# First clusters assigned by two pairs of heads, eight more tiles turned by DMA, g(h) and a*b kept in SBUF, and a new order of work

## The chip, the cores and the metric

The kernel runs on one core of a Trainium2 chip. The metric is the device time of one execution in microseconds (us): the median of the runs. Instructions run on TensorE (PE), VectorE (DVE), ScalarE (ACT) and GpSimd (POOL), each with a list of its own that it works through in order; transfers are issued from the queues of SyncE (SP), ACT and POOL.

## The reference

Everything is float32. There are 2 batches of 8 heads, 768 tokens, 64 columns per head, and 16 clusters per head; the two mixtures that follow work on all 1536 tokens of 512 columns.

```python
# attention: a token looks only at tokens of its own cluster
q_assign = argmax(einsum('bhsd,hcd->bhsc', q/|q|, c/|c|), -1)    # k_assign likewise
scores = where(q_assign == k_assign, (q @ k.T) / 8, -1e9)
x = softmax(scores) @ v                 # heads side by side: 1536 x 512
# first part: w_in 512 x 2048, w_out 2048 x 512
h = x @ w_in
g = where(h >= 1, h, where(h <= -1, 0, (h + 1)**2 / 4))
x = g @ w_out
# second part: w1, w2 512 x 1024, w3 1024 x 1024, w_out 1024 x 512
h = ((x @ w1) * (x @ w2)) @ w3
out = h @ w_out
```

## The kernel before, in words

**The pieces.** Two heads make a pair, 2 x 64 = 128 rows of SBUF. A unit u (0 to 7) is a batch and a pair: 0 to 3 are batch 0, 4 to 7 batch 1. A unit has two groups of 384 query rows, and a group has six tiles (two heads, three times 128 query rows), so there are 96 tiles s of 128 query rows x 768 keys; 0 to 47 are batch 0.

**Precision.** A float32 operand is split into a high part (rounded) and a low part (what is left); a product is three passes, high x high, high x low, low x high (`PASSES`). The copies at L347 (ACT) and L349 (DVE) make high parts, the subtractions at L352 (POOL or DVE) low parts. The names `X`, `G`, `whl`, `k`, `q`, `phl` and `pt` are such pairs.

**The start.** The centroids are loaded, normed (L419 to L432) and turned (`cT`). All four pairs of k and of q of batch 0 are loaded into `kq0` on SP's queue. `a_mm` (L511) writes the cluster logits of all pairs into one PSUM tile `sc` of 768 columns, first for k and then for q, and `a_hot` makes one-hot rows in steps over 768 columns: turn in 32 x 32 blocks (L525), maximum over 16 clusters (L531), comparison with it (L538), turn back (L543), a product with the triangle `tri` on PE (L547), and the mask (L551). The mask goes to `mask0`, and `kq_fill` copies 16 rows of it per head by DMA into rows 64 to 80 of `kq2`. There a score of two different clusters gets a term so large that its exponential is zero. While PE has nothing else, `idle_mm` (L459) multiplies the identity with itself, 80 times.

**One tile.** `s_mm` (L798) makes scores in PSUM, first from `k` and `q`, then from `kq2` with the mask rows; `s_max` (L806) takes the row maximum on DVE, `s_bias` (L811) scales it on POOL, `s_exp` (L819) is the exponential P on ACT. P is then turned so that the keys lie on the partitions. Either on PE (`s_pT`, L836, six products with the identity into the tile's own PSUM), and then a copy out (L347 or L349, and L352 for a low part); or P stays in PSUM, is split into `phl` (two buffers in batch 1), and a DMA transpose (L866, on SP's queue) turns it into `pt`. `PE_EVERY = (1, 3)` says which: every tile of batch 0 and every third of batch 1 by PE. `pv` (L907 and L915) multiplies P with V for a group into `av`; there x is multiplied by 1/r and split into `X0`.

**The mixtures.** The tokens of batch 0 are block 0, those of batch 1 block 1. A product of block 0 is 12 matmuls of 384 columns (`mm4`, L1198) into one of the PSUM tiles `mo`: three of them in batch 1's attention, one before. Three steps follow for h: Relu into `tmp` (L1206), square (L1214, L1216), and `h_max` (L1222), which writes g(h) back into `mo`; then `add_split` makes the two parts of `G` from `mo` and frees it. `ab_mul` does the same with a*b. Block 1 uses sums of matrix quarters and seven half-size products instead of eight (L1450). The weights arrive as words of twice the size, and DVE and POOL make floats of them (L1051 to L1084); w3 and w_out of the second part are multiplied beforehand into `wp` (L1142).

**What sets the order.** The `add` calls list every piece of work with the engines it may run on. `ORDER` is a string in which two letters name one piece and which of its engines does it. `plan.order()` reads it, and the pieces are issued in that order, each engine's list in the same order. No scheduler runs when the kernel is built; the string is the whole order.

Of the kernel before, what the change touches and what calls it, by code (L numbers as in the profile page):

```python
# [38 lines left out]
    "##%%%(%*%:#*#,#%#8#(#4%#%@%>%<#<#@#B&*#.#0#2&8&-#L%,&(&>&;&F&7&D#c#P;@&0#R#6#a;N;Z;i%.#:#k%B&N&P&@#Z$(;J%0%2"  # L39
    "%4%6$2#J#y#_#e&4;B&T#u#|%D%8$6#F$B&<;u%i&L#D$0&H&X$P&.$:$@$%#i;P;]%F%H%J%L%N$Z$V$>;D&2;e;R;k#o$c$F;_&J;T$T$."  # L40
    "#X#s;F#q#H$J&B;V$4$D$y;m$|;X$L&V;w;H;L;o*H*J*L*a*T*V$H*X*m$<$u$_$m*c*e<,<:*o*q*Z#g#>$X$g$w;y;a*N$]#w$i;q*s*]"
    "$8#N;c*g$e;s*P;g<%<.$#*S*i#]$N$k$a#m*u*`<<<><@<H*k<D<B&R<F*y*|<T+,$,$R$q+.*w$*$o$s#T#V+H+#+%+(+T<0<2;|<J+0+2"
    "+4<4<L<N+*+6<6<8+8<#+a&k+J<(+@&Z<V+c+L+N+m+P+V+:+e<c<_<P<R<X<o+g+X&^&`<Z&f+Z+]+<+R+_+y&g<]<a+|+o+q+><e,,+i<q"
    "<*=%&s,#,%+s+u,(+l,.+B,0,2&v<g<i<k+D=8,4,H+F<s<u<w+w,*,6,a,T<y<|,J,L&a&c,@,V,c,X=(,N,P=:=H,Z=*&j,m=,=.=0,e,g"
    ",i,]<m=<,8,:=>=2,R=B,_,k=V=J,y,|-#,o,q=g=L=@=D=N-%,s=y=#=4=6-H-,,<,>=P-.-J-(,u%R=R=T=F,w>0=X-L-0-+-2&|=Z=]&z"
    "-N=a-a-T(6=i-8=_=c,B-V>>((>*-P-4-c=e-:,D,F=|-X-Z>2-e-S-7&q-g>4&m>#-m=k(-=m=o=q(*(2-]-i&o-@(.-_>H=u-o-q>%>6=s"
    "($-k&w>N>(>8-s>,(%.,-y(>(4-<->-|..-u.H(<>..J>@>B>a.#.0.%>q.2.4.(>D>:>F%P><=w-w-B>J>L>P?%.8.:(B.+-E.L.N.P(8>R"
    ">T>V>k?6.6(A>^>_%T-F>c>e>X>Z(0%k%m.T>s.@>g.V.X.Z>u>w>y.R>|?#(:?(?H>i>m.<.].a.>.c.e._.g(H.y.m>o?*.o.|/#.q?0?8"
# [24 lines left out]
    "OZO#O/P6P(9X9ZO%O(9R9T9]9_PsPX*@*BO0P8P:P<P+8y8|9a9cOHP>PuQ<P@PZP]*D*F9#PaPw9(9*9eOJOa9g9iOL9kOcP_PcPBQ>9mOf"
    "OgPDOiOkQXPg9s9u9w9y9oQFOn9qP,P0P2Oo:6PePyQ@QBPiPkQZP|Q#P.9|Q]Q%Q(:8PN:#:%:::<Q|:(QDQHQJ:DPPPmQ_Po:>:@:F:HR>"
    ":JQaPFPSQ*:B:RQMQN:0R#PH:LR,PJPT:T:NQcPr:P:*R@RBRa:V:XR%QhQi:aPL:,:.:2:c:Z:]:_:e:g:4QeQ,Q.QPQRR(RDR*R.Q0Q2Q4"
    "Q6RFR0R2R4:i:k:m;#QT:oQ8Q:RHRJ;%QkRLRk:qS#;(;*QV:s:uR6RNQmQsQo;2:x:y:|QqRc;,QuR9;.QwR:R<S.QyRPRmReRXS&RpS)Rg"
    "RRRZR^RUS@SJS];0;:SyT#TPTaT%RVRqRiR_;4;6;8RtT5TNS|T=TLTTS0S3RuRwSBRzT^T)T9;<T;T+S*S,S4S6S:SMSNTfSESFSH;>TRS="
    "S>TWT7T,T_R|SgTyT@S_SbSPSeT|U(U*TYT[V2TuTCSjU-SlThT/SVSsTdTqV4TDT1TGU0U4U9U;T3SSSXU=U.U@V;STS8SZTmU#TIV=U&VB"
    "T?VFU?V?V@VKScV6WDSvTKVIV9TpWFXVUDSmSoSqU3VMTiSwUFWHU7UHVVTlTtULWLUSUTUCVDXZUVTwUcUeUJUgUXWJUNUZUiVOVRVPU]Um"
    "U_UkWNWPUoUPUaUwUyX]UqXXVfU|V$UtWTWXW]WRV_V%VZViWZWiX|YiV(V*W_UuVTV,VXVgV.V]Y0WwX`VkXaV0XcWqVmVuVwVoVaWaWdW%"  # L80
    "WfXhXjXkYkWmVcVqVyW(W*XmY%XoV|WVW0XqXeW|VsW,W#WsX#W.YwZ,W2W4YmWoX*W:W<W>WkY#W6W8YoXtXuW@XBXEWBYsYyWyX%Y4X.X0"
    "Z:XwXyWgY~Z(Y2X(X8X:Z/X2X4Y@XFXHX<Z1XJZHZJYBX>X@WuX,YDZ*Z<Z?Z6YGXLYHX6Z#Z%ZQZXYqZMZRZNZTZV[Z[]Z^ZaYvY(Y*Y6Y8"
    "Y,Y<Y:YJXNXPZfYLXRZZZ_YNXTYPYTZ8Z@Z2Z4]m[`YRZjZk[bYVYXYZZD[d[e[gZgZCZdY.]%ZF[kZmZ|[mY>Y]]p]r[p[t[q[iY_]|YaZu"
    "ZqYcYeYg]5Zo^#^%^0[%[(](Zw[.]wZs]6[#[2[4^3^5[w[y[F]D[6[*[,[<[H]F]H[8^>[J[v^(]s^,[|[:^L]K]L[?^N__[L[N^A[@]y^*"
    "[B[D^U^C^P^]_a^.]*].Zy]8^S]$^V]u^X^[[0`q^a_h[P[R^f^g_i^:^6]:],^i]2^q^k]<[T]>a%[V_l^<_c^m]N[X]B]c^c]Q^8^D]0^H"
# [55 lines left out]
def cluster_attention_moe_kernel(  # L141
# [223 lines left out]


    LATE = 8.0
    W_AFTER = [("al",0,"q",3)]
    V_AHEAD = 4
    AHEAD = 16  # L370
    U_DVE = 4
# [1344 lines left out]
```

## Time and profile before

| | |
|---|---|
| median of the runs | 736.93 us (736.58 to 737.46, 3 runs) |
| the profiled execution | 738.52 us, its span 736.80 us |
| PE busy | 721.2 us, 98% of the span |
| DVE busy | 629.2 us, 85% |
| ACT busy | 445.2 us, 60% |
| POOL busy | 284.0 us, 39% |

The span is the stretch from the first to the last recorded instruction; 1.7 us of the execution lie around it. A view by stretches shows for each engine how long it was busy, and the clock granted to TensorE as a part of its full speed. The view of one engine in order of time shows each group of like instructions with its start, the time it took, and in brackets how long the engine stood before it and what ended that wait. The chain of waits follows the work that ended last back from step to step.

### The profile page before, as it was taken

The page shows a single profiled execution, that of the slowest core. Times are in us where ns is not written, and L with a number is a line of the kernel's source. Part 1 is how long each engine was busy: PE and PEld are TensorE (multiplying, and loading weights), DVE is VectorE, ACT ScalarE, POOL GpSimd, SP SyncE. Part 2 cuts the span into 40 slices and gives each one's busy share as a digit, 9 for nine tenths or more (in the row PEclk, how much of TensorE's full clock was granted, in tenths as well). Part 3 has the DMA queues.
Part 4 walks back from the last instruction along what each step waited for, and adds up shares of the span by engine and source line. Part 5 has one row for each costly group of instructions (what it writes and reads, how often), then busy time and mean ns, then how long its engine had stood idle before and what let it go on. Part 6 is the DMA issues. An engine that isn't in the chain of part 4 may idle for free.

```text
span 736.8 us, 12150 instructions
## 1 busy us (share of the span) xinstructions
PE 721.2 (98%) x4273; PEld 638.4 (87%) x4273; DVE 629.2 (85%) x1153; ACT 445.2 (60%) x836; POOL 284.0 (39%) x358
## 2 busy tenths in 40 slices
PE   6999999999989999999999999999999999999997
PEld 3976666566589999999999999999999999999997
DVE  6999988998878889999999998659988878999950
ACT  6589887767666678785886675323665435444311
POOL 4332235122433523463354424222744343178601
PEclk9999999999999999999999999999999999999999
DMA  8354777575486697888869796544131312221212
GB/s 330 102 185 137 204 239 236 187 221 205 135 157 179 131 177 205 181 213 215 223 178 249 205 206 181 130 151 147 47 94 50 101 44 73 67 62 58 87 49 81
DMA packets 100973, 112.76 MB, mean 153 GB/s; under 512 B 61488, under 2 KB 69680, under 8 KB 100912
## 3 DMA queue, kind: packets, MB, share of 16 engines
q1 hardware_dynamic: 78768, 52.48, 28.6%
q10 hardware_dynamic: 22144, 59.52, 26.9%
q8 instruction: 33, 0.54, 0.3%
q14 instruction: 28, 0.23, 0.1%
HBM read 73.70 MB, written 20.19 MB: 127 GB/s over the span
## 4 chain that ended last, share of the span: by engine, by line
PE 76%; DVE 2%; DMA 2%; ACT 2%; issue 0%; POOL 0%; ACTq 0%; DVEq 0%
PE mo L1198 35%; PE sc L1450 7%; PE sc L1198 7%; PE sc L798 6%; PE mo L1450 6%; PE av L915 3%; PE mo L1142 3%; PE sc L836 3%; PE av L1450 2%; PE av L1198 1%; DMA pt<-phl 1%; PE av L907 1%; PE mo L893 1%; ACT P L819 0%; DMA wd<-wf 0%; DMA wf<-wd 0%
## 5 line engine op out<-in xcount | busy, mean ns | idle before, releaser
L1198 PE MATMUL mo<-X,whl 128*128 128x384 f32 x900 | 165.8, 339 | 0.0
L1198 PEld LDWEIGHTS mo<-X,whl 128*128 128x128 f32 x900 | 157.2, 189 | 1.9 <-issue 0.9
L1198 PE MATMUL mo<-G,whl 128*128 128x384 f32 x660 | 121.6, 337 | 0.0
L1198 PEld LDWEIGHTS mo<-G,whl 128*128 128x128 f32 x660 | 114.9, 188 | 1.1 <-DVE wf L1061 0.3
L806 DVE TENSOR_REDUCE nm<-sc 128x1 f32<-128x768 f32 x96 | 89.7, 952 | 15.4 <-PE sc L798 14.0
L352 POOL TENSOR_TENSOR whl<-wf,whl 128x512 fp32r<-128x512 f32 x54 | 70.7, 1312 | 74.2 <-DVE whl L349 38.0
L1084 POOL TENSOR_TENSOR wf<-wf,w 128x512 int32<-128x512 int32 x32 | 42.6, 1332 | 84.3 <-DVE wf L1067 21.8
L819 ACT ACTIVATE P<-sc,nm 128x768 f32<-128x768 f32 x64 | 57.1, 897 | 18.6 <-POOL nm L811 11.4
L811 POOL TENSOR_SCALAR nm<-nm 128x1 f32<-128x1 f32 x96 | 24.0, 250 | 99.0 <-DVE nm L806 93.2
L1142 PE MATMUL mo<-wo,wf 128*128 128x512 f32 x128 | 57.8, 594 | 0.3 <-POOL wf L1084 0.3
L347 ACT ACTIVATE whl<-wf 128x512 fp32r<-128x512 f32 x68 | 42.5, 628 | 24.5 <-PE mo L1198 17.6
L798 PE MATMUL sc<-k,q 128*128 128x512 f32 (+1 forms) x192 | 55.1, 368 | 2.1 <-ACT pt L347 2.1
L347 ACT ACTIVATE pt<-sc 128x768 f32<-128x768 f32 (+1 forms) x53 | 41.8, 808 | 20.4 <-PE sc L836 16.7
L836 PEld LDWEIGHTS sc<-ident,P 128*128 128x128 f32 x384 | 43.7, 141 | 11.9 <-issue 4.6
L836 PE MATMUL sc<-ident,P 128*128 128x128 f32 x384 | 50.2, 274 | 2.2 <-ACT P L819 2.2
L798 PE MATMUL sc<-kq 80*128 80x512 f32 (+1 forms) x192 | 49.8, 341 | 0.1
L1051 ACT ACTIVATE wf<-w 128x512 f32<-128x512 f32 x64 | 42.5, 672 | 6.3 <-DMA w<-in_w_in_dram 4.2
L1198 PE MATMUL sc<-G,whl 128*128 128x384 f32 x252 | 46.0, 337 | 0.0
L1067 DVE SCALAR_TENSOR_TENSOR wf<-w,wf 128x512 uint32<-128x512 uint32 x64 | 44.6, 701 | 1.0
L1142 PEld LDWEIGHTS mo<-wo,wf 128*128 128x128 f32 x128 | 23.5, 190 | 24.2 <-issue 22.8
L1198 PEld LDWEIGHTS sc<-G,whl 128*128 128x128 f32 x252 | 44.2, 188 | 0.0
L352 POOL TENSOR_TENSOR wh<-ws,wh 128x256 fp32r<-128x256 f32 x44 | 33.5, 775 | 18.0 <-DVE wh L349 7.6
(222 smaller groups left out, 1496.6 us busy)
## 6 DMA issues: line engine op xcount, KB each, us to landing
wf<-wd ACTq DMA_DIRECT2D x64, 256.0 KB, 2.7
w<-in_w_out_dram ACTq DMA_DIRECT2D x24, 512.0 KB, 4.3
wd<-wf SPq DMA_DIRECT2D x48, 256.0 KB, 3.1
w<-in_w3T_dram ACTq DMA_DIRECT2D x16, 512.0 KB, 4.1
w<-in_w_in_dram ACTq DMA_DIRECT2D x16, 512.0 KB, 4.1
w<-in_w_dram ACTq DMA_DIRECT2D x16, 512.0 KB, 4.1
wf<-wp ACTq DMA_DIRECT2D x16, 256.0 KB, 3.0
kq<-in_kT_dram SPq DMA_DIRECT2D x8, 384.0 KB, 4.3
```

The source lines that it names most:

```text
L347: nc.scalar.activation(out=out, in_=in_, func=AF.Copy)
L352: (nc.gpsimd if e == "POOL" else nc.vector).tensor_tensor(out=out, in0=a, in1=b, op=ALU.subtract)
L798: nc.tensor.matmul(ps[:, n], q[0:n_rows, q0:q0 + 128], k[0:n_rows, n], start=first, stop=not first)
L806: nc.vector.tensor_reduce(out=nm, in_=T[("sc", b), s], axis=AX.X, op=ALU.max, negate=True)
L819: nc.scalar.activation(out=new(("P", b), s).rearrange("p n s -> p (n s)") if by_pe(s) else T[("sc", b), s], in_=T[("sc", b), s], func=AF.E ...
L836: nc.tensor.transpose(T[("sc", b), s][:, c], p[:, c], ident)
L1051: nc.scalar.activation(out=T["wf", i], in_=T[w64, i].bitcast(F32)[:, :, 1], func=AF.Abs)
L1067: nc.vector.scalar_tensor_tensor(out=w, in0=T[w64, i][:, :, 1], scalar=0xC0000000, in1=w, op0=ALU.bitwise_and, op1=ALU.bitwise_or)
L1084: nc.gpsimd.tensor_tensor(out=w, in0=w, in1=T[w64, i].bitcast(I32)[:, :, 0], op=ALU.add)
L1142: nc.tensor.matmul(acc, w[:, k4 * 128:(k4 + 1) * 128], wo2[:, hf * 4 + k4], start=(hf == 0 and k4 == 0), stop=(hf == 1 and k4 == 3),)
L1198: nc.tensor.matmul(acc, w[:, a, k4 * 128:(k4 + 1) * 128], rhs(c, k4), start=(first and k4 == 0 and n == 0), stop=(last and k4 == 3 and n = ...
L1450: nc.tensor.matmul(ps, lhs(av, a, k), rhs(bv, c, k), start=k == 0 and n == 0, stop=k == 1 and n == 2,)
```

## The change

1. Batch 0's clusters are assigned by two pairs of heads. `a_mm` and `a_hot` get a half p: pairs 0 and 1, or 2 and 3. Its logits fill 128 partitions x 384 columns of `sc` (the two halves of the tokens side by side on the partitions), so each step has 384 columns. The mask of head 0 of pair 0 is written straight into `kq2` (`a_mask0`), without a DMA; for k it may also run on ACT (a Relu). The loads are issued as q of pair 0, k of 0, 1 and 3, q of 1, k of 2, q of 3 and 2 (before: k of 1, 2 and 3, q of 0, k of 0, q of 3, 2 and 1).
2. The Exp that loads ACT's table stands in a piece of its own (`cent_exp`), behind the square root.
3. `PE_EVERY` is (1, 6): every sixth tile of batch 1 is turned by PE, 8 tiles instead of 16; the other 40 by DMA (before 32).
4. `h_max` and `ab_mul` write into the SBUF tile `tmp`; `mo` is freed there. `add_split` then reads `tmp`, and its subtraction may run on POOL as well as on DVE: in the new order POOL does 14 of the 32 of block 0's h, and 11 of the 16 of a*b.
5. `N_IDLE` is 40, a clamp of the weights may run on POOL, and `ORDER` is a new string.

```diff
-    PE_EVERY = (1, 3)
+    PE_EVERY = (1, 6)
...
-    N_IDLE, N_IDLE1 = 80, 0
+    N_IDLE, N_IDLE1 = 40, 0
...
-        nc.scalar.activation(out=cs["all"][:, 0, 380:381], in_=rt, func=AF.Exp, scale=-1.0)
+
+    def cent_exp(e):
+        nc.scalar.activation(out=cs["all"][:, 0, 380:381], in_=cs["ss"], func=AF.Exp, scale=-1.0)
...
+            n = a_cols(("sc", 0), key, p)
+            for x in range(NG):
+                for i in range(2):
+                    r, j = 64 * x + 32 * i, 2 * p + i
                     nc.tensor.matmul(
-                        ps[32 * j:32 * j + 32, n], cT[:, j, :], raw_ap(b, w, j, "a")[:, n], start=True, stop=True
+                        ps[r:r + 32, n], cT[:, j, :], raw_ap(b, w, j, "a")[:, cols(x)], start=True, stop=True
                     )
...
+    def a_mask0(w, x):
+
+        def fn(e):
+            key2 = ("a2", 0, w, 0)
+            a_mask(
+                e, w, T[("kq2", 0), (0, 0)][D:HR, "kq".index(w), cols(x)],
+                T[("sc", 0), key2][64 * x:64 * x + C, a_cols(("sc", 0), key2, 0)], 64 * x,
+            )
...
     def h_max(name):
         def fn(e):
             h = mo(name, False)
-            nc.vector.scalar_tensor_tensor(out=h, in0=T["tmp", name], scalar=1.0, in1=h, op0=ALU.min, op1=ALU.max)
+            t = T["tmp", name]
+            nc.vector.scalar_tensor_tensor(out=t, in0=t, scalar=1.0, in1=h, op0=ALU.min, op1=ALU.max)
...
-            nc.vector.tensor_tensor(out=ab, in0=T["tmp", tname], in1=ab, op=ALU.mult)
+            nc.vector.tensor_tensor(out=T["tmp", tname], in0=T["tmp", tname], in1=ab, op=ALU.mult)
...
-                    add(("hm", blk, m, g), {"DVE": 0.47}, tg + 1.1, h_max(nm), [("hs", blk, m, g)], frees=[("tmp", nm)])
-                    add_split("h", nm, tg + 1.7, lambda a, sl=sl, g=g: G()[:, sl, a, cols(g)], [("hm", blk, m, g)] + war, mo_ring)
+                    add(("hm", blk, m, g), {"DVE": 0.47}, tg + 1.1, h_max(nm), [("hs", blk, m, g)], frees=[(mo_ring, nm)])
+                    add_split("h", nm, tg + 1.7, lambda a, sl=sl, g=g: G()[:, sl, a, cols(g)], [("hm", blk, m, g)] + war)
```

DVE's list at the start, before the change, from the last subtraction for q and k on (`amx` is the maximum over the clusters, `phl` the one-hot rows, P the turned logits):

```order
L352 TENSOR_TENSOR q_100<-kq_116,kq_103 64x768
L349 CAST k_97<-kq_116 64x768
L525 STREAM_TRANSPOSE P_106<-sc_177 128x768
L531 TENSOR_REDUCE amx<-P_106 128x48
L538 TENSOR_TENSOR phl_108<-P_106,amx 128x768
L543 STREAM_TRANSPOSE phl_108<-phl_108 128x768
L525 STREAM_TRANSPOSE P_107<-sc_177 128x768
L551 TENSOR_SCALAR mask_115<-sc_178 128x768
L531 TENSOR_REDUCE amx<-P_107 128x48
L538 TENSOR_TENSOR phl_109<-P_107,amx 128x768
L543 STREAM_TRANSPOSE phl_109<-phl_109 128x768
L551 TENSOR_SCALAR mask_115<-sc_177 128x768
```

Now the same place, up to the mask of the first score; ahead of it stand the turns and the maximum of the first halves of k and q (L549 twice, L555), behind it the rest of the second halves with operations on the weights between them:

```order
L562 TENSOR_TENSOR phl_109<-P_107,amx 128x384
L555 TENSOR_REDUCE amx<-P_108 128x24
L567 STREAM_TRANSPOSE phl_109<-phl_109 128x384
L549 STREAM_TRANSPOSE P_106<-sc_178 128x384
L562 TENSOR_TENSOR phl_110<-P_108,amx 128x384
L549 STREAM_TRANSPOSE P_107<-sc_178 128x384
L567 STREAM_TRANSPOSE phl_110<-phl_110 128x384
L555 TENSOR_REDUCE amx<-P_106 128x24
L584 TENSOR_SCALAR mask_116<-sc_178 128x384
L1111 TENSOR_SCALAR wo_118<-wo_118 128x512
L584 TENSOR_SCALAR kq_103<-sc_178 16x384
```

What moved: the two masks of all heads stood behind ten steps of 768 columns; the first mask row that a score needs now stands behind steps of 384 columns for two pairs, and the steps of the other two pairs are woven between weights.

PE's list at the switch from batch 0 to batch 1, before the change (`mo<-X,whl` is a product of block 0, `sc<-ident,P` turns a tile, `sc<-k,q` and `sc<-kq` are scores), from tile 50's scores to tile 52's:

```order
L798 MATMUL sc_1746<-k_97,q_100 128x512
L798 MATMUL sc_1746<-k_97,q_100 128x256
L798 MATMUL sc_1746<-kq_103 128x512
L798 MATMUL sc_1746<-kq_103 128x256
L1198 MATMUL mo_122<-X_75,whl 128x384 x12
L1198 MATMUL mo_1740<-X_75,whl 128x384 x12
L836 MATMUL sc_1746<-ident,P_105 128x128 x6
L798 MATMUL sc_1745<-k_97,q_100 128x512
```

And now:

```order
L853 MATMUL sc_1736<-k_98,q_101 128x512
L853 MATMUL sc_1736<-k_98,q_101 128x256
L853 MATMUL sc_1736<-kq_104 128x512
L853 MATMUL sc_1736<-kq_104 128x256
L1254 MATMUL mo_123<-X_75,whl 128x384 x12
L1254 MATMUL mo_1730<-X_75,whl 128x384 x12
L1254 MATMUL mo_1731<-X_75,whl 128x384 x12
L853 MATMUL sc_1735<-k_98,q_101 128x512
```

What moved: the transposes on PE are gone from this place, and a third product of block 0 stands in front of the next scores.

PE's list behind the last product of P and V of batch 1, now, the last six of the eleven products of block 0 that come before the first product of block 1 (L1507, before L1450); fourteen stood there before the change:

```order
L1254 MATMUL mo_123<-X_75,whl 128x384 x12
L1254 MATMUL mo_1731<-G,whl 128x384 x12
L1254 MATMUL mo_1730<-X_75,whl 128x384 x12
L1254 MATMUL mo_1731<-X_75,whl 128x384 x12
L1254 MATMUL mo_123<-G,whl 128x384 x12
L1254 MATMUL mo_1730<-G,whl 128x384 x12
L1507 MATMUL sc_5077<-X_1871,whl 128x384 x6
```

What moved: three products of block 0 left the stretch between the two blocks for earlier places.

## Rows read from the trace of the kernel before

**Rows 1.** Busy us, share of the span and instructions of each engine.

```profile
PE 721.2 (98%) x4273; PEld 638.4 (87%) x4273; DVE 629.2 (85%) x1153; ACT 445.2 (60%) x836; POOL 284.0 (39%) x358
```

**Rows 2.** Stretches: length, busy PE PEld DVE ACT POOL, PEclk, DMA share, GB/s.

```profile
0.00:42.00 42.00, 35.12 (x258) 29.57 (x259) 33.05 (x60) 26.84 (x42) 15.05 (x23) 1.00 0.62 215
42.00:195.00 153.00, 151.44 (x798) 94.22 (x796) 137.71 (x230) 118.94 (x210) 46.73 (x72) 1.00 0.62 198
...
222.00:733.00 511.00, 510.64 (x3088) 494.08 (x3086) 437.42 (x832) 281.66 (x554) 212.65 (x250) 1.00 0.53 136
```

**Rows 3.** PE in order of time at the start: start, length, operation, [wait].

```profile
9.74 2.79 PE L511 MATMUL sc<-kq,cT 128*32 128x512 f32 x16 [0.92 <-DMA kq<-in_kT_dram]
12.46 2.47 PE L459 MATMUL av<-ident 128*128 128x128 f32 x14
14.86 1.50 PE L511 MATMUL sc<-kq,cT 128*32 128x256 f32 x16
...
18.10 2.84 PE L459 MATMUL av<-ident 128*128 128x128 f32 x24
...
26.84 0.60 PE L798 MATMUL sc<-k,q 128*128 128x256 f32 x2
...
28.00 0.52 PE L798 MATMUL sc<-k,q 128*128 128x512 f32 x2
...
45.02 4.09 PE L907 MATMUL av<-pt,vn 128*64 128x384 f32 x24
```

**Rows 4.** ACT at the start: the first copies of q.

```profile
8.76 1.71 ACT L347 ACTIVATE kq<-kq 64x768 fp32r<-64x768 f32 x2 [3.74 <-DMA kq<-in_qT_dram]
```

**Rows 5.** DVE at the start.

```profile
5.06 0.22 DVE L426 SCALAR_TENSOR_TENSOR rt<-ss,rr,rt 128x1 f32<-128x1 f32 x1 [1.35 <-ACT P L419]
...
9.64 1.94 DVE L352 TENSOR_TENSOR q<-kq,kq 64x768 fp32r<-64x768 f32 x2 [1.67 <-ACT kq L347]
...
14.60 2.11 DVE L538 TENSOR_TENSOR phl<-P,amx 128x768 bf16<-128x768 f32 x1
...
20.32 1.20 DVE L538 TENSOR_TENSOR phl<-P,amx 128x768 bf16<-128x768 f32 x1
...
38.71 1.82 DVE L806 TENSOR_REDUCE nm<-sc 128x1 f32<-128x768 f32 x2
```

**Rows 6.** DVE by line and shape: count, busy us, mean ns, idle before and why.

```profile
L806 DVE TENSOR_REDUCE nm<-sc 128x1 f32<-128x768 f32 x96 | 89.7, 952 | 15.4 <-PE sc L798 14.0 <-PE sc L836 0.4 <-ACT pt L347 0.3
L1067 DVE SCALAR_TENSOR_TENSOR wf<-w,wf 128x512 uint32<-128x512 uint32 x64 | 44.6, 701 | 1.0
L1055 DVE TENSOR_SCALAR wf<-wf 128x512 f32<-128x512 f32 x64 | 26.8, 426 | 2.8 <-ACT wf L1051 2.0 <-POOL tmp L883 0.7
L1222 DVE SCALAR_TENSOR_TENSOR mo<-tmp,mo 128x384 f32<-128x384 f32 x32 | 17.8, 555 | 2.1 <-POOL tmp L1216 1.1 <-ACT tmp L1214 0.8
```

**Rows 7.** The chain of waits, in order of time: start, length, what.

```profile
192.28 1.98 PE sc L836 x18
...
202.55 9.75 DMA pt<-phl
...
317.87 0.81 PE sc L836 x6
```

**Rows 8.** PE and ACT in order of time at the switch of batches.

```profile
195.85 0.62 PE L798 MATMUL sc<-k,q 128*128 128x512 f32 x2 [1.60 <-ACT pt L347]
...
212.39 0.81 ACT L347 ACTIVATE phl<-sc 128x768 f16<-128x768 f32 x1 [3.54 <-DMA pt<-phl]
...
214.61 1.00 PE L836 MATMUL sc<-ident,P 128*128 128x128 f32 x6 [2.17 <-ACT P L819]
```

**Rows 9.** Stretches behind that wait, of batch 1, and between the blocks.

```profile
215.00:219.00 4.00, 4.00 (x18) 3.81 (x17) 3.83 (x8) 3.42 (x8) 2.47 (x4) 0.57 0.60 121
...
200.00:480.00 280.00, 277.83 (x1752) 261.93 (x1750) 252.05 (x442) 191.93 (x353) 112.19 (x133) 0.99 0.79 188
481.30:510.90 29.60, 29.60 (x173) 29.56 (x173) 21.75 (x41) 8.12 (x18) 8.14 (x8) 1.00 0.48 145
```

**Rows 10.** DMA from 200 to 480 us: SP's queue, packets, MB, share.

```profile
q1 hardware_dynamic: 64624, 30.71, 51.9%
```

**Rows 11.** The tile `pt`: issue to landing of its transposes.

```profile
DMA to landing us min/median/max: 3.7/4.8/10.2
```

More of the change, by code (lines that the diff above doesn't have):

```diff
@@ L44 @@
[L44 to L48, printed above, removed]
@@ L367, in cluster_attention_moe_kernel @@
     LATE = 8.0
-    W_AFTER = [("al",0,"q",3)]
+    W_AFTER = []
     V_AHEAD = 4
@@ L504, in raw_load, with a_cols, a_mm @@
         return fn
-    def a_mm(b, w, js):
-        def fn(e):
-            ps = new(("sc", 0), ("a", b, w))
-            for n in splits(("sc", 0), ("a", b, w)):
-                for j in js:
+    def a_cols(ring, name, p):
+        if p is None:
+            return slice(0, S)
+        o = 0 if splits(ring, name)[0].stop == 512 else 256
+        return slice(o, o + TG)
+    def a_mm(b, w, p):
+        def fn(e):
+            key = ("a", b, w, p)
+            ps = new(("sc", 0), key)
+            if p is None:
+                for n in splits(("sc", 0), key):
+                    for j in range(NP):
+                        nc.tensor.matmul(
+                            ps[32 * j:32 * j + 32, n], cT[:, j, :], raw_ap(b, w, j, "a")[:, n], start=True, stop=True
+                        )
+                return
+            n = a_cols(("sc", 0), key, p)
+            for x in range(NG):
+                for i in range(2):
+                    r, j = 64 * x + 32 * i, 2 * p + i
@@ L597, in cluster_attention_moe_kernel @@
             if b:
-                add(("ap", w), {"DMA": 0.5}, t + 2.5, a_put(w), [("ah", b, w, 5)], frees=[(("P", 0), ("m", w))])
+                add(("ap", w), {"DMA": 0.5}, t + 2.5, a_put(w), [("ah", b, w, 5, None)], frees=[(("P", 0), ("m", w))])
     def dma_of(b):
@@ L661, in fn @@
             dma = dma_of(b)
-            mask = mask1 if b else f(mask0)
             kq2 = f(T[("kq2", b), (u, h)])
@@ L667, in fn @@
                 dma(out=q1[rows(1 - h)], in_=kq2[0:D, 1])
-            dma(out=kq2[D:HR], in_=mask[hd * C:(hd + 1) * C])
+            if b:
+                dma(out=kq2[D:HR], in_=mask1[hd * C:(hd + 1) * C])
+                return
+            for x in range(NG):
+                r = 64 * x + 32 * (j % 2) + C * h
+                dma(out=kq2[D:HR, :, cols(x)], in_=f(mask0)[r:r + C, j // 2])
         return fn
@@ L1105, in chunk @@
             add(("wabs", i), {"ACT": 0.56}, t - 9.0, absv, [("wl", i)], [] if dst is not None else [("wf", i)], behind="wf")
-            add(("wc", i, 0), {"DVE": 0.34}, t - 8.6, clamp, [("wabs", i)])
+            add(("wc", i, 0), {"DVE": 0.34, "POOL": (1.92, LATE)}, t - 8.6, clamp, [("wabs", i)])
             add(("wc", i, 1), {"DVE": 0.34}, t - 8.2, rebase, [("wc", i, 0)])
@@ L1452, in fn @@
                         )
-            add((L + "p", U, p), {"PE": 1.045}, t + 1.05 * off.get(p, n), fn, [done[av]] + b_done[bv] + room(p), [(R3, (U, p))], [hold[av]])
+            add((L + "p", U, p), {"PE": 1.052}, t + 1.05 * off.get(p, n), fn, [done[av]] + b_done[bv] + room(p), [(R3, (U, p))], [hold[av]])
     def t_sums(key, t, vals, dst, war):
```

241 lines of the change are left out of this document (134 added, 107 removed).

## The prediction, made before the changed kernel was run

> **What bounds the kernel now.** I read the engines' busy shares first, then the span in stretches, then the two ends of it and the one gap in its middle. TensorE (PE) is busy for 721.2 of 736.8 us [rows 1]. The stretches show where the other 15.6 us are [rows 2]: in the first 42 us PE is busy for 35.12, and much of that is filler, the 80 identity products of `idle_mm`; from 42 to 195 it misses 1.56 us of 153; from 222 to 733 it misses 0.36 us of 511. So outside the start and the few us around 195 to 219 the end of the kernel is the sum of what PE has to do. A us taken from PE's list, or a us by which its dense part begins earlier, comes off the end, as long as VectorE (DVE), ScalarE (ACT), GpSimd (POOL) and the transfers keep up. That is the question to put to every part of the change.
>
> **The start (term A).** The dense part begins at about the first product of P and V, at 45.02 us; the first score stands at 26.84 [rows 3]. Before it the chain is: loads of q and k, cluster logits, seven cluster steps per tensor, masks. The loads land one per us: ACT gets the fourth at 8.76, PE the fifth at 9.74 [rows 3, 4]. By the same spacing the new order of loads brings q and k of the first pair of heads at 5.8, 6.8, 7.8 and 9.7 us. The centroids stop being late: DVE waited 1.35 us for a second ACT table that the norm does not need [rows 5], and that Exp now stands behind the square root without the norm waiting for it.
>
> DVE takes its list in order, so I count its rows. Two subtractions come first (0.97 us each [rows 5]); the second needs ACT's copy of k of head 1, the fifth of five copies of 0.85 [rows 4], from 5.8 to about 10.2 with the waits for k; so DVE begins on the clusters at 11.2. A step on 384 columns does not occur in the trace; a DVE operation of 384 columns takes 0.555, one of 768 columns 0.952 [rows 6], so I take 0.55 for each. From the order of DVE in the change: twelve such steps, one weight operation (0.43) and one mask (0.55) are 7.6 us, and the small product between them 0.3: the first score can start at 19.1. The next three scores wait on PE behind the product of the second pair's q clusters, which needs twelve more DVE rows: seven of 0.43 to 0.70 for weights and steps alike, in sum 6.9 us, then 0.3: 26.4, against 28.00 for the second score before [rows 3]. Seventeen rows later, 10.2 us by the same durations, comes the fifth row maximum: 36.3, against 38.71 [rows 5]. From there to the first product of P and V both orders have the same work on ACT (two exponentials, one weight, two copies).
>
> So the gain is between 2.4 us (that maximum) and 7.6 (the first score alone). One step speaks for less: the comparison with the maximum took 2.11 us for 768 columns the first time and 1.20 the second [rows 5]; at 1.06 for a half, the four that stand ahead of the fifth maximum add 2.0 and leave 0.4 of the 2.4. I take 3.0, near the maximum, which is the row closest to the end of this stretch. The end above nothing is in the rivals. The forty identity products that go cost nothing by themselves: they fill waits.
>
> **Eight tiles turned by DMA (term B).** Every sixth instead of every third tile of batch 1 is now transposed on PE: 16 become 8, 48 transposes less. Three tiles in a row took 1.98 us in the chain, 0.66 each; one tile alone 0.81 [rows 7]. That is 5.3 to 6.5 us off a list that has no gaps there; I take 5.3. DVE and ACT do the same two passes for such a tile either way. What is added is eight DMA transposes. The trace does not give the price of one in the engines' time alone; SP's queue held 51.9% of 16 engines over 280 us, 145 us, for 36 transposes and all its plain transfers [rows 10], so one takes at most 4.0 us and eight at most 32: the share there would go from 0.79 [rows 9] to at most 0.91. They fit. If they were late PE would have other products to do, but only in its fixed order; that is a rival.
>
> **The switch of batches (terms C and D).** At 195.85 PE waited 1.60 us for ACT to copy the last two tiles of batch 0, one after the other [rows 8]. In the new order one of the two copies is on DVE and 1/r's product stands in the gap; 0.9 is left: C is -0.7, between 0 and -1.6. Then the costliest gap: a DMA transpose issued at 202.55 landed 9.75 us later [rows 7]; ACT stood for it 3.54 us with its next copy, the exponential of tile 51 stood behind that, and PE, at the transposes of tile 51, waited 2.17 us [rows 8]. Behind it PE ran at a granted clock of 0.57 on average for 4 us, in the level 1.2 GHz for most of it [rows 9]: 4 x 0.43 = 1.7 us more. The order shows that tile 51 is now turned by DMA and that a third product of block 0 stands between the scores of tiles 51 and 52. Those scores need the buffer of tile 50, free about 1.8 us after the same landing (copy 0.81, subtraction 0.95). If the landing takes 9.75 us again PE gets there at about the same moment. Of the 3.9 us I take 2.9.
>
> **Keeping g(h) and a*b in SBUF** moves 25 subtractions to POOL (14 of h, 11 of a*b) and frees the PSUM tile one or two steps earlier. PE does not wait there now [rows 2], so this is worth nothing by itself; DVE, at 252 of 280 us [rows 9], is relieved. If POOL's slower subtractions were late, the matmuls that read G are several products behind; I cost it at nothing, with the next term as its bound.
>
> **What the new order brings of its own (term E).** A new order has its own small waits. The old one has 1.56 + 0.36 us of them outside the places named; I add 1.5, from 0 to 8 (two gaps like the one at 212).
>
> Sum: -3.0 - 5.3 - 0.7 - 2.9 + 1.5 = -10.4 us. The profiled execution took 738.52 for a span of 736.80 and would come to 728.1; the median of the runs is 1.6 below it, so the forecast is 736.9 - 10.4 = 726.5 us.
>
> **Rivals.** *A slow PE at the start.* Before, the first cluster products took 2.79 us and the same work later 1.50; fourteen identity matmuls took 2.47 us and later twenty-four 2.84 [rows 3]: the beginning of PE's activity runs at about half speed. With forty fillers less PE's stretch from 26.4 us could be like that: nine scores and six tiles of transposes before the first product of P and V, 10.3 us at full speed, would take 20.6 and end where they end now, A = +0.7. Time 726.5 + 3.7 = 730.2. Against it: 31 of the forty still stand ahead of those scores.
> The Trainium skill has the rule (TensorE: Matmul & The Clock Gate, "HAM oscillation"): an array that waits between short stretches falls back to half clock and pays for each restart. By that rule this rival would be the case if the waits between the tiles are long; the drop after the wait at 212 agrees (clock 0.57).
>
> *The next block starves.* Between the last product of P and V and the first of block 1 there were 14 products of block 0, 29.6 us; in the new order there are 11, 23.1. Loads of the second block's x wait for that last product. If their sums need the whole 29.6 us, PE waits 6.5: 733.0. Against it: DVE was busy 21.75 of those 29.6 us [rows 9], so it has room, and the first product's operand comes earlier in its list.
>
> *Slower than before: transposes that stop PE.* Five tiles of six now go through two buffers of halves and a DMA. Median landing is 4.8 us, the longest 10.2 [rows 11]; with copy and subtraction a buffer is taken for 6.6 us, so a tile every 3.3, while 48 tiles in 280 us need one per 5.8. At a landing of 9.75 it is 5.75: no room left, and each such tile can stop PE as tile 51 did, for 3.9 us. One of 32 did so before. Three stops eat the gain; if six of forty do it, the time is 726.5 + 23.4 = 750.
>
> *It does not do what it says*: the gaps return elsewhere and the sum of PE's list is all that is gained, less new waits of the same size: no change, 737.
>
> **Numbers.** Forecast 0.66; slow start 0.12; starved block 0.13; slower 0.06; no change 0.03. The range 720.5 to 733.5 takes in the first three: its low end is a start nearer to 7.6 and the transposes at 0.81, its high end the starved block. A measurement of this kernel can tell 0.2%, 1.5 us. Faster by more: 0.90 (the first three less a little for mixtures); within: 0.04; slower: 0.06.
>
> **What the next profile would show.** A: first score near 19, the next three near 26, first product of P and V near 42. B: 336 transposes of P, and each of the other 40 tiles landing within some 6 us. D: no wait over 1 us and no drop of the clock between 195 and 222. PE's total down by some 10 us with filler included. I am wrong if PE's idle time after 45 us grows by more than 4 us, or if the first product of P and V is not before 44.

## The result

The changed kernel takes 725.49 us (median of 4 runs, 724.05 to 726.77), the kernel before 737.19 beside it: ratio 0.9837, 95% interval 0.982 to 0.9854, 11.7 us less (10.8 to 13.3 by the interval). The forecast was 726.5. The profiled execution took 725.32 for a span of 723.6. Of one kernel further down, `pe6_keep`, two of the five executions (756.37 and 759.51 us) were in a slow state and are left out of its figures.

The page's first part, after ([rows 1] before):

```profile
PE 704.4 (97%) x4144; PEld 617.9 (85%) x4145; DVE 615.9 (85%) x1134; ACT 465.5 (64%) x870; POOL 285.3 (39%) x358
```

The stretches, with the columns of [rows 2] and [rows 9]; the fifth is the one whose clock was 0.57 before:

```profile
0.00:42.00 42.00, 28.94 (x195) 21.11 (x195) 33.10 (x73) 34.06 (x53) 15.00 (x25) 1.00 0.60 209
42.00:195.00 153.00, 151.76 (x791) 93.32 (x790) 136.76 (x225) 122.68 (x209) 47.10 (x71) 1.00 0.62 201
195.00:219.00 24.00, 24.00 (x142) 21.09 (x141) 21.26 (x36) 17.22 (x33) 9.84 (x16) 1.00 0.82 181
222.00:720.00 498.00, 496.53 (x3005) 479.46 (x3003) 422.94 (x801) 288.11 (x571) 210.90 (x244) 1.00 0.57 142
215.00:219.00 4.00, 4.00 (x25) 3.96 (x25) 3.34 (x6) 3.43 (x8) 3.47 (x5) 1.00 1.03 250
```

The third of them before the change:

```profile
195.00:219.00 24.00, 20.99 (x116) 17.58 (x117) 18.07 (x30) 14.86 (x29) 8.45 (x13) 0.93 0.76 153
```

PE's idle time between 195 and 219 is gone (3.01 us before, 24.00 of 24.00 busy now), and the clock from 215 to 219 is whole. Behind 222 PE misses 1.47 us instead of 0.36.

PE in order of time at the start, after ([rows 3]):

```profile
20.01 0.60 PE L853 MATMUL sc<-k,q 128*128 128x256 f32 x2
...
26.30 0.64 PE L853 MATMUL sc<-k,q 128*128 128x512 f32 x2
...
28.42 0.62 PE L853 MATMUL sc<-k,q 128*128 128x256 f32 x2 [1.12 <-DVE nm L861]
...
31.52 0.87 PE L891 MATMUL sc<-ident,P 128*128 128x128 f32 x6 [1.33 <-DVE nm L861]
...
42.23 4.09 PE L962 MATMUL av<-pt,vn 128*64 128x384 f32 x24
```

The first product of P and V stands 2.79 us earlier (42.23 against 45.02). It follows waits that the old start did not have: the fillers cover fewer of them.

PE's transposes by line, before and then after (count, busy, mean; idle before, and its releaser):

```profile
L836 PE MATMUL sc<-ident,P 128*128 128x128 f32 x384 | 50.2, 274 | 2.2 <-ACT P L819 2.2
```

```profile
L891 PE MATMUL sc<-ident,P 128*128 128x128 f32 x336 | 43.9, 275 | 1.6 <-DVE nm L861 1.3 <-ACT P L874 0.3
```

The span is 13.2 us shorter. Of that 2.8 lie ahead of the first product of P and V; the 48 transposes are up to 6.3; the waits and the clock at the switch of batches (3.0 us of idle time and 1.7 of slow clock) are 4.7; 1.1 of new waits goes off, and 0.5 is left over, of which 0.3 is idle time between 42 and 195 (1.24 us instead of 1.56). The profile of before was one of its longer executions (738.52), so between medians it is 11.7.

### The profile page after: what moved, and what is told of

The parts are those of the page before. It is cut to its first block, busy times and chain, and to the rows that moved or that the text cites. A ratio compares the mean times of both kernels' runs of the same rounds, so it can differ in the third digit from the quotient of the medians.

```text
span 723.6 us, 11965 instructions
## 1 busy us (share of the span) xinstructions
PE 704.4 (97%) x4144; PEld 617.9 (85%) x4145; DVE 615.9 (85%) x1134; ACT 465.5 (64%) x870; POOL 285.3 (39%) x358
## 4 chain that ended last, share of the span: by engine, by line
PE 89%; DVE 4%; ACT 3%; DMA 2%; issue 1%; SPq 0%; POOL 0%; ACTq 0%; POOLq 0%; DVEq 0%
PE mo L1254 36%; PE sc L1507 9%; PE sc L853 9%; PE mo L1198 7%; PE mo L1507 5%; PE sc L891 5%; PE sc L1254 5%; PE av L962 4%; PE av L970 3%; PE av L1507 2%; PE av L1254 2%; DMA vn<-phl 1%; DMA kq<-in_qT_dram 1%; DVE nm L861 1%; ACT pt L347 1%
## 5 line engine op out<-in xcount | busy, mean ns | idle before, releaser
L1254 PE MATMUL mo<-G,whl 128*128 128x384 f32 x732 | 133.2, 337 | 0.0
L1254 PEld LDWEIGHTS mo<-G,whl 128*128 128x128 f32 x732 | 126.6, 188 | 0.9 <-DVE X L352 0.3
L352 POOL TENSOR_TENSOR whl<-wf,whl 128x512 fp32r<-128x512 f32 x48 | 63.3, 1319 | 73.1 <-ACT whl L347 44.6
L347 ACT ACTIVATE whl<-wf 128x512 fp32r<-128x512 f32 x76 | 47.5, 627 | 29.4 <-PE mo L1254 11.8
L874 ACT ACTIVATE P<-sc,nm 128x768 f32<-128x768 f32 x56 | 50.1, 898 | 10.6 <-POOL nm L866 5.5
L891 PEld LDWEIGHTS sc<-ident,P 128*128 128x128 f32 x336 | 37.9, 141 | 12.5 <-issue 4.9
L891 PE MATMUL sc<-ident,P 128*128 128x128 f32 x336 | 43.9, 275 | 1.6 <-DVE nm L861 1.3
L874 ACT ACTIVATE sc<-sc,nm 128x768 f32<-128x768 f32 x40 | 34.7, 868 | 15.5 <-POOL nm L866 15.4
L352 DVE TENSOR_TENSOR phl<-sc,phl 128x768 f16<-128x768 f32 x40 | 38.1, 952 | 5.6 <-ACT phl L347 5.2
L853 PEld LDWEIGHTS sc<-k,q 128*128 128x128 f32 x192 | 31.4, 189 | 12.2 <-DVE nm L861 3.0
```

What stands on the lines that cost most here:

```text
L347: nc.scalar.activation(out=out, in_=in_, func=AF.Copy)
L352: (nc.gpsimd if e == "POOL" else nc.vector).tensor_tensor(out=out, in0=a, in1=b, op=ALU.subtract)
L853: nc.tensor.matmul(ps[:, n], q[0:n_rows, q0:q0 + 128], k[0:n_rows, n], start=first, stop=not first)
L874: nc.scalar.activation(out=new(("P", b), s).rearrange("p n s -> p (n s)") if by_pe(s) else T[("sc", b), s], in_=T[("sc", b), s], func=AF.E ...
L891: nc.tensor.transpose(T[("sc", b), s][:, c], p[:, c], ident)
L1254: nc.tensor.matmul(acc, w[:, a, k4 * 128:(k4 + 1) * 128], rhs(c, k4), start=(first and k4 == 0 and n == 0), stop=(last and k4 == 3 and n = ...
```

## The experiments

All were timed in turn with the kernel before, whose medians there were 737.4 to 737.9; "changed" is the changed kernel's ratio of 0.9837. A us figure behind a ratio is the ratio's distance from 1, or from 0.9837, times 737.4.

**The two halves apart.** `new_start` has the changed start and the old rest, `old_start` the other way round. Each order was cut at the first product of P and V; pieces of work that both halves had are done where the first half has them.

```diff
 # new_start, in the changed kernel
-    PE_EVERY = (1, 6)
+    PE_EVERY = (1, 3)
-            nc.vector.scalar_tensor_tensor(out=t, in0=t, scalar=1.0, in1=h, ...)
+            nc.vector.scalar_tensor_tensor(out=h, in0=T["tmp", name], scalar=1.0, in1=h, ...)
 # and ORDER: new up to pv(0, 0), old from there
```

> The kernel before with the new start alone: clusters by two pairs of heads, the new order up to the first product of P and V, forty fillers, the old order behind it, every third tile of batch 1 on PE, g(h) and a*b in PSUM. If PE's list behind that product sets the end, the 2.8 us by which it came earlier in the changed kernel's profile (42.23 against 45.02) come off whole: 737.2 - 2.8 = 734.4, ratio 0.996. Rival: what begins earlier waits later (VectorE has only 14% of the time free in batch 0), and less than 1 us is left: 736.2 or more.

> Everything of the change but its start: old assignment of the clusters with 768-column steps and the old order up to the first product of P and V, 80 fillers, then the new order, every sixth tile on PE, g(h) and a*b in SBUF. By my sum it keeps the terms behind the start: 737.2 - 8.9 = 728.3 (the measured 11.7 less 2.8), first product of P and V at 45. Rival, the two parts hang together (the new order behind the start only fits the work that the new start has done): 731 or more, with waits of PE in batch 0.

Measured: `new_start` 733.35, ratio 0.9941 (0.9922 to 0.9961), 4.4 us; its first product of P and V stands at 41.91. `old_start` 731.72, ratio 0.9913 (0.9897 to 0.993), 6.4 us; first product at 44.94. Together 10.8 of the 12.0 that the ratio of the whole is worth: the halves nearly add up. `old_start` came out in its rival's range, not in mine. Its trace shows no wait in batch 0 beyond the usual, but PE waiting 1.4 us at the last product of P and V for a transpose (landing 7.8 us, the longest there).

The 4.4 us of `new_start` are not the start alone. Its profiled execution (730.88, the shortest of six) has the first product of P and V 3.1 us earlier and a span 7.6 us shorter. At the transposes of tile 51, which are still on PE there, PE waits 0.4 us instead of 2.17 (in the view of waits: us in total, times, longest), and the clock from 215 to 219 is 1.00:

```profile
PE sc L891 <- ACT P L874: 0.4, 1, 0.4
```

So a part of the gain at the switch of batches came with the start. Neither half was taken apart further: the pairs of heads, the order of the loads, the Exp, the mask without a DMA and the forty fillers were changed together.

**Tiles by DMA in the old order.** `before_51` gives one tile to the DMA, `before_pe6` all eight, with ACT's copy moved into the place of the transposes; `pe6_keep` leaves copy and subtraction where they were.

```diff
-        return s % PE_EVERY[s // NU] == 0
+        return s % PE_EVERY[s // NU] == 0 and s != 51      # before_51
-    PE_EVERY = (1, 3)
+    PE_EVERY = (1, 6)                                      # before_pe6, pe6_keep
```

> The kernel before with one tile, 51, turned by DMA instead of PE; nothing else is moved. If the wait of 2.17 us at 212 and the slow clock behind it are in every execution, its price is 2.17 + 1.7, and with the six transposes that go 4.5 us come off: 732.7, and the clock from 215 to 219 is 1.00. If that wait was an accident of the profiled execution (a landing of 9.75 us against a median of 4.8), only the transposes go, 0.66: 736.5. If the wait only moves to tile 52's scores, which need the buffer of tile 50 after the same landing: 736.5 too, with a wait of 2 us at L798 in the profile.

> The kernel before with eight tiles of batch 1 more turned by DMA (every sixth on PE instead of every third), the order otherwise as it was. My terms B and D: 48 transposes of 0.11 to 0.14 us less are 5.3 to 6.5, and the stop at tile 51 goes with 2 to 3.9: 737.2 - 8 = 729, between 727 and 732. Rival, the transposes stop PE: DMA transposes through two buffers land late, several stops of 2 to 4 us, 735 to 745.

> The kernel before with the same eight tiles by DMA as in the run that came to 748.0, but ACT's copy and VectorE's subtraction of such a tile stay where they stood in the old order (in that run I had put them one step earlier, into the place of the transposes); only PE's transposes go and a DMA transpose follows the subtraction. Theory 1, my placing made ACT and VectorE stand: now the stops are gone and 727 to 733 is left. Theory 2, the old order has no room for a landing of 4 to 5 us between a tile's subtraction and what needs its buffer, wherever the copy stands: 742 to 750 again.

Measured: `before_51` 739.74, ratio 1.0025 (1.0006 to 1.0044). `before_pe6` 748.02, 1.0143 (1.012 to 1.0167). `pe6_keep` 745.79, 1.0108 (1.0091 to 1.0126). All slower, where my terms said 4.5 and 8 us faster. Moving the copy back helps by some 2.6 us, far from theory 1's 727 to 733; theory 2 fits. PE behind tile 51 in `before_51`:

```profile
213.54 0.62 PE L798 MATMUL sc<-k,q 128*128 128x512 f32 x2 [1.06 <-DVE phl L352]
215.80 2.34 PE L1198 MATMUL mo<-X,whl 128*128 128x384 f32 x12 [1.30 <-DVE G L352]
219.70 2.38 PE L1198 MATMUL mo<-X,whl 128*128 128x384 f32 x12 [1.55 <-DVE G L352]
235.96 0.35 PE L915 MATMUL av<-pt,vn 128*64 128x384 f16 x2 [1.71 <-DMA pt<-phl]
```

The one wait of 2.17 us became four smaller ones of 5.6 in sum: for tile 50's buffer, for VectorE's parts of G that stand behind it, and for the fifth DMA transpose of the batch, tile 53's (issued at 227.79, landed at 235.82). The longest stop of `pe6_keep`, by engine in order of time:

```profile
440.96 0.81 ACT L347 ACTIVATE phl<-sc 128x768 f16<-128x768 f32 x1 [3.94 <-DMA vn<-phl]
...
441.80 0.96 DVE L352 TENSOR_TENSOR phl<-sc,phl 128x768 f16<-128x768 f32 x1 [3.72 <-ACT phl L347]
...
442.81 1.01 PE L798 MATMUL sc<-k,q 128*128 128x512 f32 x2 [3.33 <-DVE phl L352]
```

This is the mechanism as these rows show it: there are two `phl` buffers, V's own transpose uses them too, and ACT takes its list in order. Its copy waits for a landing, VectorE's subtraction for the copy, PE's next scores for the PSUM tile that the subtraction frees. Whatever is behind them on ACT and VectorE waits too.

**Eight tiles back to PE in the new order.**

```diff
-    PE_EVERY = (1, 6)
+    PE_EVERY = (1, 3)
 # ORDER: transposes in the place of the tile's copy, copy and subtraction five entries later
```

> The changed kernel with the old every-third rule again: eight tiles of batch 1 go back from the DMA to PE (six products with the identity, copy and subtraction behind them), all else in the new order. If in this order the eight DMA transposes are hidden and PE's list is what counts, as my term B has it, 48 transposes of 0.11 to 0.14 come back: 725.5 + 5.3 to 6.5 = 731.4, ratio 0.992. Rival (from the run that gave the kernel before the same eight tiles by DMA and lost 10.6): DMA transposes cost waits here as well, and taking eight back costs less than 2 us, or gains: 727.5 or less.

Measured: 742.24, ratio 1.0065 (1.0043 to 1.0087), 16.8 us over changed; both theories missed it. From 222 to 480 us PE is idle 8.2 us against 1.5 in the changed kernel, mostly in scores that wait for a tile's last subtraction:

```profile
PE sc L853 <- DVE pt L352: 4.9, 4, 1.9
```

As I read it, a tile by PE holds its PSUM tile longer, and the new order left no room for that. So this run does not price the transposes, and in neither direction did a swap without a new order pay.

**The price of PE's list by itself.** Identity products, which nothing reads, at the eight places.

```diff
+    for s in range(51, 96, 6):
+        for i in range(6):
+            add(("pad", s, i), {"PE": 0.12}, 0.0, idle_mm, ["c_const"])
```

> The changed kernel with 48 identity products more on PE, six at each of the eight places where the transposes of tiles 51, 57, ..., 93 would stand; nothing reads them, and the tiles still go by DMA. This prices 48 transposes on PE's list alone. If PE's list has no gaps there, as term B says: 725.5 + 48 x 0.11 to 0.14 = 731 to 732. Rival, VectorE and the DMA are the bound of this stretch by now and PE has room: 727 or less.

Measured: 738.04, ratio 1.0001 (0.9987 to 1.0016), 12.1 us over changed. PE by line from 200 to 482 us:

```profile
L464 PE MATMUL av<-ident 128*128 128x128 f32 x96 | 12.2, 277 | 0.0
```

and the stretch from 200 to 480, with the columns of [rows 9]:

```profile
200.00:480.00 280.00, 280.00 (x1791) 264.19 (x1788) 247.64 (x422) 202.43 (x371) 115.94 (x141) 1.00 0.81 197
```

An identity product is two matmuls in the records, a transpose only one: the 48 are 96, 0.109 us from start to start, 10.4 us of PE, not the 5.3 that I had expected. PE was busy for 280.00 of the 280 us from 200 to 480, and what it owed at 482 came on the end. The first product of P and V stood at 44.85 here, 2.6 us late, though the start is the changed kernel's; 10.4 and 2.6 are 13.0, of the 13.3 by which this profile's span is longer. In the executions whose clock held the 10.4 stand nearly alone: the three of twelve with a mean clock of 0.999 or 1.000 took 734.35, 735.50 and 736.26 us, 8.9 to 10.8 over changed. The late start goes with PE's clock, from 30 to 36 us:

```profile
30.00:36.00 6.00, 4.66 (x22) 4.15 (x21) 5.84 (x11) 4.29 (x8) 2.02 (x4) 0.58 0.25 86
```

In the changed kernel's profile that stretch has 1.00, with the same 4.67 us busy. So this start holds the clock in some executions and loses it in others.

**The fillers.**

```diff
-    N_IDLE, N_IDLE1 = 40, 0
+    N_IDLE, N_IDLE1 = 0, 0
```

> The changed kernel without any of the forty identity products at the start. If VectorE's list sets the first scores there, the fillers only cover waits: 725.5, within 1 us, first product of P and V at 42. The rival of the prediction, a slow clock after idle time: PE's work between 20 and 42 us (scores and transposes, some 10 us at full speed) runs up to twice as long, and the end comes 2 to 8 us later: 728 to 733, with a granted clock under 1 before 42 us.

Measured: 729.52, ratio 0.989 (0.9874 to 0.9907), 3.9 us over changed: the rival. The start in two stretches:

```profile
14.00:36.00 22.00, 13.05 (x45) 8.24 (x46) 17.15 (x34) 13.88 (x24) 5.11 (x7) 0.50 0.40 143
36.00:42.00 6.00, 5.53 (x23) 4.16 (x21) 4.11 (x9) 3.83 (x7) 1.80 (x3) 0.59 0.51 174
```

A granted clock of 0.50 is the lower level, 1.2 GHz, and PE stays there for 22 us with waits between its work; the first product of P and V comes at 47.10, 4.9 late. The Trainium skill (TensorE: Matmul & The Clock Gate, "HAM oscillation") says that an array with waits between short stretches falls back; by that rule this run is the slow start that the prediction had as a rival, and the trace agrees (0.50). That the clock explains all of the 3.9 us is not shown: of the four executions one has a mean clock of 1.000 and took 729.07, as did another with 0.984. A mean clock can miss a slow beginning: [rows 2] give 1.00 for a stretch in which the cluster products took 2.79 us, and 1.50 later [rows 3].

**g(h) and a*b in SBUF.** `before_sbuf` makes this edit in the kernel before (`h_max` and `ab_mul` write `tmp`, low parts on VectorE); `pe6_sbuf` adds the eight DMA tiles; `lo_dve` is the changed kernel with POOL's 25 subtractions on VectorE.

```diff
 # before_sbuf and pe6_sbuf, in the kernel before (ab_mul likewise; pe6_sbuf: PE_EVERY = (1, 6) too)
-            nc.vector.scalar_tensor_tensor(out=h, in0=T["tmp", name], scalar=1.0, in1=h, ...)
+            nc.vector.scalar_tensor_tensor(out=t, in0=t, scalar=1.0, in1=h, ...)
 # lo_dve, in the engine of 25 entries of ORDER
-("hl", 0, m, g) and ("abl", 0, m, g): POOL
+("hl", 0, m, g) and ("abl", 0, m, g): DVE
```

> The kernel before with the eight more DMA tiles (which alone came to 748.0) and with g(h) and a*b kept in SBUF, the low parts still on VectorE, the old order of work. In the run without SBUF the products of block 0 waited for a PSUM tile of mo that the two parts of G still held (PE behind DVE G L352: 6.6 us in 6 waits). Theory 1, that hold is what turned the DMA tiles into stops, and I was wrong to value the SBUF part at nothing: it now comes to 731 to 735, and these waits are gone. Theory 2, the stops come from ACT's and VectorE's lists standing behind the two phl buffers, whatever holds mo: 745 to 749, and only a new order helps.

> The kernel before with g(h) and a*b of block 0 kept in SBUF (tmp) and the PSUM tile freed there, low parts on VectorE, old order, every third tile on PE. My prediction costed this part at nothing: 737 to 738. Rival: tmp has only four buffers, each is now held for two steps more, and what asks for the next one waits (with the eight DMA tiles this edit cost 7 us more): 740 to 745, with PE behind tmp in the waits. The third possibility, that freeing mo early is worth something by itself, would show as 735 or less.

> The changed kernel with the 25 subtractions of h and a*b in block 0 that POOL does back on VectorE (g(h) and a*b stay in SBUF), the order otherwise the same. VectorE gets 25 x 0.55 = 14 us more between 200 and 480 us, where it is busy 246 of 280. If it has room there, as I costed it (nothing), 725.5 to 727. If not, PE waits for what VectorE owes: up to 14 us, and 730 or more says that POOL's part was needed.

Measured: `before_sbuf` 743.88, ratio 1.008 (1.0067 to 1.0093), 5.9 us slower; `pe6_sbuf` 754.81, 1.0223 (1.0203 to 1.0243), 16.4 slower, which is the sum of `before_sbuf` and `before_pe6` (5.9 and 10.5): theory 1 falls. `lo_dve` 733.58, 0.9936 (0.9915 to 0.9957), 7.3 over changed. The rival's buffers of `tmp` are not what `before_sbuf` waits for: PE stands behind `tmp` once, for 0.3 us. What did change is how long VectorE's operations take. The parts of G on VectorE, in nanoseconds (shortest/median/longest), first before, then `before_sbuf`:

```profile
L352 DVE TENSOR_TENSOR G<-mo,G x55: 542/551/558, 209.3 to 679.6; 128x384 fp32r<-128x384 f32 x55
```

```profile
L352 DVE TENSOR_TENSOR G<-tmp,G x40: 542/556/2104, 209.3 to 440.4; 128x384 fp32r<-128x384 f32 x40
L349 DVE CAST G<-tmp x16: 346/576/1424, 214.1 to 439.8; 128x384 fp32r<-128x384 f32 x16
```

Reading `tmp` instead of PSUM, the same subtraction took up to 2104 ns. Of these 56 operations 20 took over 600 ns, all of them beside an operation of POOL; beside none the longest was 558. From PSUM none took over 558, beside POOL or not. From 200 to 480 us VectorE was busy for 260.92 us instead of 252.05 [rows 9]:

```profile
200.00:480.00 280.00, 275.15 (x1714) 255.00 (x1711) 260.92 (x435) 192.98 (x354) 116.79 (x133) 1.00 0.77 186
```

PE's idle time there is 2.7 us more than before (4.85 against 2.17), in waits for exponentials and last subtractions; that the longer operations cost all of the 5.9 is argued, not shown. In the changed kernel two of its 36 took over 600 ns, in `lo_dve` three of 54. There 12 of the 36 and 18 of the 54 ran beside POOL, in `before_sbuf` 40 of the 56; why so few of those are long in the new order is open. The Trainium skill (SBUF — State Buffer, "Who interferes with whom") says that a VectorE instruction with two SBUF inputs contends with a GpSimd instruction that reads SBUF; the subtractions agree with it (2104 against 558 ns). Of the 20 long operations 8 are casts, which have one SBUF input and which that sentence does not speak of: they took at most 360 ns alone, and up to 1424 beside POOL.

**Less on VectorE's list at the start.**

```diff
 # w_late, ORDER: wc(0, 1), wc(0, 2), wc(1, 0) to wc(1, 3), wc(2, 0) on DVE
-between the cluster steps
+behind smax(8)
```

> The changed kernel with seven VectorE operations on the weights (3.6 us), which stand between the cluster steps at 19.9 to 26.6 us, moved behind the row maximum of the ninth tile; what follows from them moves too. If VectorE's list sets the start, as my term A counts it, the second masks, the fifth maximum and the first product of P and V (42.2) come up to 3.5 us earlier, and the end 1 to 3.5 us: 722 to 724.5, which would beat both kernels. Rival, ACT's list or the loads set it by now, or VectorE owes the 3.6 us later: first product of P and V at 41.5 or later, end 725 to 728.

Measured: 753.37, ratio 1.0218 (1.0198 to 1.0238). PE at the end of the start:

```profile
41.96 4.16 PE L962 MATMUL av<-pt,vn 128*64 128x384 f32 x24
71.36 0.90 PE L891 MATMUL sc<-ident,P 128*128 128x128 f32 x3 [25.24 <-ACT P L874]
```

Two readings. The first product of P and V came 0.27 us earlier, not 3.5, so VectorE's list alone does not set it. VectorE ended the one-hot rows of the second pair at 24.07 us instead of 26.10, but PE's product with the triangle behind them began only at 25.98 instead of 26.28. Ahead of it on PE stand the first tile's transposes, which waited for ACT's exponential, and five identity products:

```profile
24.15 0.87 PE L891 MATMUL sc<-ident,P 128*128 128x128 f32 x6 [0.56 <-ACT P L874]
24.86 1.28 PE L463 MATMUL av<-ident 128*128 128x128 f32 x10
25.98 0.33 PE L574 MATMUL sc<-phl,tri 128*128 128x384 bf16 x1
```

And 24 further entries that follow from the seven were moved behind the ninth maximum with them, among them four loads of weights on ACT's queue, which need the buffers that the operations hold. So ACT stood for these loads, with the exponentials behind it (us in total, times, longest):

```profile
ACT wo L1107 <- DMA w<-in_w_out_dram: 16.9, 3, 8.3
ACT wf L1107 <- DMA w<-in_w_in_dram: 6.8, 1, 6.8
```

No version here beat the changed kernel.

## Why the prediction was right, step by step

**What bounds it** was right. 10.4 us more on PE's list in batch 1 came on the end (`pe_pad`, 8.9 to 10.8 where the clock held), and a later beginning of the dense part moved the end: 4.9 us in the profile of `no_fill`, 3.9 us between medians.

**Term A** (-3.0; 2.4 to 7.6) measured -2.8 in the trace and -4.4 (2.9 to 5.8) for `new_start`, which holds a part of D too. The rows came near the count: first score 20.01 (19.1), next three from 26.30 (26.4), fifth maximum at 35.52 (36.3), first product of P and V at 42.23. A step of 384 columns took 0.50 to 0.64 (0.55), once 0.87. But the cause that I gave, VectorE's list, sets only part of it. Without seven of its operations the end of the start hardly moved. PE's own list holds it as much (`w_late`, 25.98). Behind the second pair's masks, as I read the trace, the round from score to maximum to exponential to copy sets the pace; its waits are the 1.12 and 1.33 us above, which my count contained without naming. No run changes that round alone.

"The forty identity products that go cost nothing" fits the trace, whose clock is 1.00 without them, though no run put them back; it hid what the other forty are worth, 3.9 us. The rival "a slow PE at the start" (0.12) did not occur in the changed kernel's profile; it did in `pe_pad`'s, whose first product of P and V at 44.85 is about where the rival put it (45.7).

**Term B** (-5.3) is right in the trace of the whole (up to -6.3), and wrong as a part that stands by itself. "They fit" was argued from the share of the DMA engines, which indeed went only from 0.79 [rows 9] to 0.85. The sign that each tile lands within some 6 us failed (five of the 40 took longer, up to 8.4 us), yet PE's longest wait in batch 1 is 0.84 us. What decides is the time from a copy to the landing of the transpose two tiles before, on two in-order lists. In the old order the rival "transposes that stop PE", to which I gave 0.06, is what the edit does: 8.0 to 10.5 us slower. The new order is what makes the eight tiles free, and I had priced it at nothing but a loss.

**Terms C and D** (-3.6 in sum) measured -5.2. Of C's wait of 1.60 us [rows 8] 0.30 is left:

```profile
193.57 0.61 PE L853 MATMUL sc<-k,q 128*128 128x512 f32 x2 [0.30 <-ACT pt L347]
```

D's 2.17 us and the 1.7 of slow clock are gone. (The 4.7 above counts from 195 us on and so only 0.84 of the 1.60.) The 1.7 is not in every execution: of the 48 of the kernel before that were timed beside these runs, 22 have a mean clock of 1.000. And D is not due to tile 51's route, as I had it: `before_51`, which changes only that, is slower, and `new_start`, which leaves the tile on PE, waits only 0.4 us there. (PE's list at the switch, shown with the change, begins with the scores of tile 51, not 50: its transposes go into the same tile, `sc_1746`.) The first transpose of batch 1 landed in 3.8 us instead of 9.75 [rows 7]. SP's queue there, before and then after:

```profile
201.93 0.53 SPq L668 DMA_DIRECT2D kq<-mask  x1
202.55 2.38 SPq L866 DMA_TRANSPOSE pt<-phl  x1
```

```profile
194.48 0.32 SPq L718 DMA_DIRECT2D kq<-mask  x1
...
200.48 1.55 SPq L921 DMA_TRANSPOSE pt<-phl  x1
```

The copies of a head's rows and mask used to be issued 0.6 us ahead of the transpose; now they are 6 us ahead. In the seven profiles with 0.6 us (before, `new_start`, `before_51`, `before_pe6`, `pe6_keep`, `before_sbuf`, `pe6_sbuf`) it landed in 9.8, 8.0, 9.0, 5.7, 9.2, 8.6 and 9.5 us, in the seven with 6 us in 3.8 each. That is an agreement of fourteen traces; no run moved these copies alone, so the cause is not shown.

**g(h) and a*b in SBUF**, costed at nothing, is the step that failed: alone it costs 5.9 us, and POOL's share of it gains 7.3 in the new order. That the sum did not suffer is luck, as two effects that I had not seen lie on opposite sides; no run prices the whole part in the new order.

**Term E** (+1.5) measured +1.1 behind 222 us. *The next block starves* (0.13) did not happen: from 480 to 500 us PE was busy for 20.00 of 20. PE's total fell by 16.8 us, not by the "some 10 us" of the signs: the transposes and the forty fillers (0.22 each) make 15 of it.

So the time was right because each place of the whole was read against the new order, where each priced term holds to within 1.6 us. The terms as measured add up to 13.2 us between two profiles; that the medians differ by 11.7, nearer to the forecast's 10.4, is due for the most part to the profile of before, which lay 1.6 us over its median. That a part gains by itself held only for the start: of the four parts put alone into the old kernel, tile 51, the eight tiles and the SBUF part each cost time.

## What to carry to other kernels

When an order is written out as a whole, price the whole against the engine that bounds it, and do not hand the gain to the edits: the route of eight tiles, swapped by itself in either direction, cost 8 to 17 us here. Ahead of giving work to a DMA, look not at the engines' share but at who waits, in order, for the buffer that the landing frees. And keep the filler products of a start until a run without them has shown what they hold up.

## What the runs showed of the hardware

- A VectorE subtraction of 128 x 384 with both inputs in SBUF took up to 2104 ns beside POOL's work, and at most 558 when one input was in PSUM.
- An identity product in float32 is two matmuls in the records (0.22 us), a transpose through the identity one (0.11).
- With the same start, PE's clock fell in one profiled execution (0.58 from 30 to 36 us, first product of P and V 2.6 us late) and held in another (1.00).
